# Block 0's attention computed transposed, and one written list of steps up to the 24th product

## The chip, the core and the metric

The kernel runs on one core of one Trainium2 chip. The metric is the device time of one execution in microseconds (us), the median of several runs. Inputs and outputs lie in the chip's main memory; the kernel moves them with DMAs into the on-chip memory, where five engines work side by side: TensorE (PE; its weight loads are PEld), VectorE (DVE), ScalarE (ACT), GpSimd (POOL) and SyncE (SP), which here issues nearly all DMAs. Each engine executes its own queue strictly in the order in which it was written, and waits on semaphores for the others.

## The reference

Three steps in a row over 8 batches x 576 rows = 4608 tokens of 512 numbers (8 heads of 64):

```
kv  = einsum('bhsd,bhse->bhde', k, v)        # 64 x 64 per batch and head
o   = einsum('bhsd,bhde->bhse', q, kv)
x   = o / sqrt(mean(o*o over 64) + 1e-6) * g_norm        # per token and head
xn  = x / sqrt(mean(x*x over 512) + 1e-6) * rms_g        # per token
y   = (silu(xn @ w_gate) * (xn @ w_val)) @ w_out         # 512 -> 1536 -> 512
out = relu(y @ w_in)**2 @ w_out2                         # 512 -> 2048 -> 512
```

All of it is float32. The two norms of one token need, per head, the sum of o*o and the sum of o*o*g_norm*g_norm; both factors are then one number per token and head.

## The kernel before, in words

**Tiles and stages.** The 4608 tokens are nine blocks of 512 (`NB`, `T`). Blocks are worked on in stages: blocks 0 and 1 first, then 2, then pairs; first all stages of the gated layer, then those of the second layer. In a stage a *product* is six matmuls of 128x128 weights with 512 tokens into one PSUM bank (`product`): every operand is split into a high and a low part, and three of the four combinations for two slices of the contraction are summed. After each product the kernel calls `tick()`, a counter in the program text by which all other work is placed between the products: `at(t, fn)` and `after(n, fn)` put a step at a tick, and `prep_q` holds the steps that prepare weights, taken one per tick or slower (`pace["prep"]`). The engines see only the order that results.

**The first stage** has no prepared weights yet. For each unit of 256 columns of the gate matrix (`g`) and of the value matrix (`v`) the steps of `prep_unit` load 1 MB of raw 64-bit words (`load`), turn them into float32 with two ScalarE instructions (`bits_1`, `bits_2`) and two VectorE instructions (`bits_3`, `bits_4`), split them (`hi` on ScalarE, `lo` on VectorE), and store the words and the split form for later (`words_out`, `put`). Units 0 to 5 are used straight from where they are made: four products to a unit. Products 1 to 24 are block 0 with units 0 to 5, products 25 to 48 block 1 with the same units.

**Block 0's attention** stands ahead of the first product. `kv_whole` sums k-v products of five row chunks in PSUM, `kv_out` copies them to `kvb`, `o_mm2` multiplies two q tiles of 128 tokens each by it (tokens on the partitions), ScalarE squares the result out of PSUM, GpSimd multiplies the squares by g_norm squared (`att_sg`), VectorE sums both over 64 columns (`att_sum`, eight instructions), forms the factors with some twenty small instructions (`att_m`, `att_r`) and multiplies (`att_y2`). `x1_T` turns each 128x128 piece with TensorE so that features lie on the partitions, `x_hi` and `x_lo` split it into the operand of the products. `keep(n)` issues n matmuls of the identity into an unused bank. Block 1's attention (`o_events(1, 1, 3, 22, True)`) is spread over ticks 1 to 24; its pieces are turned at ticks 22 and 23.

**The order around the change** in the old text: a few `prep_step()` calls (each is one time step of the list that `prep_first` makes of all units), the loads, and the calls above, one under the other at the end of `attn_moe_moe`; then the ticks. VectorE and ScalarE take what comes in that order; SP issues at most eight DMAs ahead, since each of its eight semaphores must have come back before it is used again.

## Time and profile before

| what | us |
|---|---|
| median of 3 runs | 1572.36 (1570.51 to 1572.75) |
| the profiled execution, its own time | 1572.19 |
| its span, first to last instruction | 1570.4 |
| TensorE busy in the span | 1560.2 (99%) |
| VectorE / ScalarE / GpSimd busy | 1182.2 / 727.3 / 62.9 |
| bytes moved by DMA | 463.99 MB, mean 295 GB/s |

The span starts with the first instruction; times "at 30.95" are us from there. A row of the timeline gives the start, the length, the engine, the line, the operation, what it writes and reads, and how many instructions are merged; in brackets stands how long the engine had nothing to do ahead of it and what ended that. A float32 matmul is two records in the trace, a product's matmul one, so one q tile pair of `o_mm2` (64 matmuls in the program's count, 32 of them to a tile) and one filler of `keep` show different counts in the two views. The granted clock is given as a share of 2.4 GHz: 0.50 is 1.2 GHz.

### The profile page before, as it was taken

The numbers are of one execution on the slowest core, as the hardware profiler recorded it, in microseconds if no ns is written. First come the engines' busy times: TensorE is split into PE (matmuls) and PEld (weight loads), VectorE is DVE, ScalarE is ACT, GpSimd is POOL, SyncE is SP. The second block draws the span as 40 slices with busy tenths as digits, with TensorE's granted clock in tenths as the row PEclk, the third lists the DMA queues.
The fourth block names the chain that finished last, engine by engine and source line by source line (L and its number), as shares of the span: only waits on it lengthen the run. The fifth ranks groups of instructions, "written<-read, shape, count | busy, mean of one in ns | idle before, by whom it ended". The sixth has DMA issues, their size and how long they took to land.

```text
span 1570.4 us, 23134 instructions
## 1 busy us (share of the span) xinstructions
PE 1560.2 (99%) x8800; PEld 1301.6 (83%) x8800; DVE 1182.2 (75%) x1594; ACT 727.3 (46%) x983; POOL 62.9 (4%) x50
## 2 busy tenths in 40 slices
...
GB/s 373 327 394 412 345 293 337 394 315 358 397 261 259 295 336 353 219 353 347 394 318 265 390 338 219 246 249 191 196 247 244 194 198 253 236 195 205 230 409 235
DMA packets 174926, 463.99 MB, mean 295 GB/s; under 512 B 14048, under 2 KB 47840, under 8 KB 170464
## 3 DMA queue, kind: packets, MB, share of 16 engines
...
q8 instruction: 70, 1.15, 0.3%
...
## 4 chain that ended last, share of the span: by engine, by line
PE 97%; DVE 1%; DMA 1%; ACT 0%; SPq 0%; issue 0%
PE c L807 55%; PE a L1070 21%; PE e L1070 10%; PE d L1070 5%; PE acc L1037 2%; PE ops L519 1%; PE kvps L457 1%; PE idle L1227 1%; DMA kvraw<-in_kv_dram 1%; DVE ws L231 0%; DVE wpw L176 0%; DVE wpw L170 0%; PE xps L628 0%; DVE ss L568 0%; DVE hr L883 0%; PE kvps L481 0%
## 5 line engine op out<-in xcount | busy, mean ns | idle before, releaser
L807 PE MATMUL c<-xo,wt 128*128 128x512 f32 (+1 forms) x3480 | 759.2, 379 | 0.0
L807 PEld LDWEIGHTS c<-xo,wt 128*128 128x128 f32 x3480 | 629.4, 188 | 122.9
L1070 PE MATMUL a<-ho,wt 128*128 128x512 f32 (+1 forms) x1536 | 334.1, 376 | 0.0
L715 ACT ACTIVATE ho<-hr 128x1024 fp32r<-128x1024 f32 (+1 forms) x230 | 230.8, 1006 | 204.1 <-PE a L1070 97.4
L716 DVE TENSOR_TENSOR ho<-hr,ho 128x1024 fp32r<-128x1024 f32 (+1 forms) x230 | 266.2, 1159 | 73.5 <-ACT ho L715 72.8
L1070 PEld LDWEIGHTS a<-ho,wt 128*128 128x128 f32 x1536 | 275.5, 188 | 52.8 <-DVE ho L716 0.4
L818 ACT ACTIVATE s<-c 128x512 f32<-128x512 f32 (+1 forms) x228 | 129.7, 573 | 183.7 <-PE c L807 183.3
L822 DVE TENSOR_TENSOR c<-c,s 128x512 f32<-128x512 f32 (+1 forms) x174 | 113.1, 650 | 81.0 <-PE c L807 75.7
L1070 PE MATMUL e<-ho,wt 128*128 128x512 f32 (+1 forms) x768 | 167.5, 376 | 0.0
L1070 PEld LDWEIGHTS e<-ho,wt 128*128 128x128 f32 x768 | 137.6, 188 | 26.4 <-DVE ho L716 0.3
L719 DVE TENSOR_TENSOR hr<-hr 128x1024 f32<-128x1024 f32 (+1 forms) x128 | 147.8, 1155 | 2.2
L807 PE MATMUL c<-xo,ws 128*128 128x512 f32 x576 | 135.1, 393 | 1.3 <-DVE ws L231 1.2
L807 PEld LDWEIGHTS c<-xo,ws 128*128 128x128 f32 x576 | 106.9, 188 | 25.1 <-DVE ws L231 2.0
L716 DVE TENSOR_TENSOR xo<-xr,xo 128x1024 fp32r<-128x1024 f32 (+1 forms) x58 | 67.0, 1158 | 39.5 <-ACT xo L715 39.3
L883 DVE TENSOR_TENSOR hr<-c,hr 128x512 f32<-128x512 f32 x108 | 74.7, 693 | 17.9 <-PE c L807 16.2
L1070 PE MATMUL d<-ho,wt 128*128 128x512 f32 (+1 forms) x384 | 85.0, 376 | 0.0
L1070 PEld LDWEIGHTS d<-ho,wt 128*128 128x128 f32 x384 | 68.9, 188 | 13.1
L829 DVE SCALAR_TENSOR_TENSOR hr<-c 128x512 f32<-128x512 f32 (+1 forms) x120 | 76.7, 639 | 4.0
L826 ACT ACTIVATE hr<-hr 128x512 f32<-128x512 f32 x54 | 34.2, 633 | 89.0 <-DVE hr L822 88.8
L878 ACT ACTIVATE r<-c 128x512 f32<-128x512 f32 (+1 forms) x40 | 22.1, 554 | 113.6 <-PE c L807 103.9
L231 DVE TENSOR_TENSOR ws<-wpl,ws 128x1024 fp32r<-128x1024 f32 (+1 forms) x44 | 49.6, 1128 | 31.3 <-ACT ws L224 31.0
L554 POOL TENSOR_TENSOR sq<-sq,gg_sb 128x512 f32<-128x512 f32 x32 | 49.6, 1549 | 553.7 <-ACT sq L540 538.3
...
## 6 DMA issues: line engine op xcount, KB each, us to landing
wt<-wd_g SPq DMA_DIRECT2D x150, 512.0 KB, 7.1
wt<-wd_i SPq DMA_DIRECT2D x140, 512.0 KB, 5.0
wt<-wd_p SPq DMA_DIRECT2D x140, 512.0 KB, 4.7
wt<-wd_o SPq DMA_DIRECT2D x96, 512.0 KB, 5.6
...
kvraw<-in_kv_dram SPq DMA_DIRECT2D x35, 512.0 KB, 7.4
...
```

What stands on the lines that cost most here:

```text
L231: nc.vector.tensor_tensor(out=t[:, :, 1, :], in0=quarters(st["sw"[1 - h]])[:, q], in1=t[:, :, 0, :].bitcast(F32), op=ALU.subtract)
L554: nc.gpsimd.tensor_tensor(out=heads(sg), in0=heads(sq), in1=gg_sb.rearrange("p (o d) -> p o d", o=1).to_broadcast([128, H, D]), op=ALU.mult)
L715: nc.scalar.activation(out=dst[:, 0], in_=src, func=AF.Copy)
L716: eng.tensor_tensor(out=dst[:, 1], in0=src, in1=dst[:, 0].bitcast(F32), op=ALU.subtract)
L719: eng.tensor_tensor(out=o, in0=x, in1=y, op=ALU.subtract)
L807: nc.tensor.matmul(ps, lhsT=w[:, a, kc * 128:(kc + 1) * 128], rhs=x[:, b, kc, :], start=(start and n == 0 and kc == 0), stop=(n == 2 and k ...
L818: nc.scalar.activation(out=t, in_=ps, func=AF.Copy)
L822: nc.vector.tensor_tensor(out=o, in0=ps, in1=t, op=ALU.add)
L826: nc.scalar.activation(out=hr, in_=c, func=AF.Silu)
L829: nc.vector.scalar_tensor_tensor(out=hr, in0=c, scalar=0.0, in1=c, op0=ALU.max, op1=ALU.mult)
L883: after(2, lambda: nc.vector.tensor_tensor(out=hr, in0=c, in1=hr, op=ALU.mult))
L1070: nc.tensor.matmul(ps, lhsT=w[e][:, a, d * 128:(d + 1) * 128], rhs=x[:, b, e, :], start=(i in (1, 2, 5) and q == 0 and e == 0 and a + b == 0),
```

## The change

**Transposed attention for block 0.** `ot` multiplies with kv as the stationary operand and q as the moving one, so that the result has features on the partitions and 128 tokens in the columns; no `x1_T` follows. ScalarE squares it (`sq`), VectorE copies it out of PSUM (`cp`). The new constant `w4` (128x4: a column of ones for either head, and g_norm squared for either head) is multiplied with the squares by TensorE (`s`), which gives both sums per token and head in one PSUM tile; GpSimd's four multiplications and VectorE's eight sums of block 0 are gone. The factors come out with tokens on the partitions, so ScalarE spreads them over 64 columns (`rb`, four instructions), TensorE turns them (`t`, 16 transposes), and VectorE multiplies (`x`). `x_hi` and `x_lo` then read the result from on-chip memory.

**One list.** `FIRST` names every step up to the 24th product, by engine queue order: the first string runs ahead of product 1, string k after product k. `first_op` carries a name out; `prep_first` no longer emits units 0 to 5, nor the first three steps of unit 6, and the other preparations start at tick 21 (`BEGIN_PREP`). The silu and multiply of products 1 to 24 (`s0.0`, `h0.0`, ...) are in the list as well. The fillers fall from 44 to 13. Block 1 keeps its form; its steps have other places, and its 16 transposes now stand together after product 23.

The core of the diff:

```
+BEGIN_PREP = 21
+EARLY = 6
+FIRST = (
+    "kv.0 kv.1 keep.5 km0.0 kv.2 keep.1 km0.1 kv.3 keep.1 km0.2 kv.4 q.0 keep.1 km0.3 q.1 km0.4 load.0 kvb.0 "
+    "keep.1 ot.0 ot.1 q.2 sq.0 q.3 cp.0 b1.0 gr keep.1 ot.2 kv.5 b2.0 ot.3 load.1 sq.2 b3.0 sq.1 s.2 sq.3 cp.2 "
+    "s.1 b4.0 s.3 kv.6 s.0 cp.3 hi.0 km1.0 kv.7 m.0 b1.1 keep.1 km1.1 kv.8 r0.0 b2.1 keep.1 km1.2 kv.9 r1.0 q.4 "
+    "keep.1 km1.3 cp.1 q.5 rb.0 km1.4 rb.3 lo.0 load.2 t.0 rb.1 t.3 kvb.1 x.0 t.1 rb.2 o1.0 x.3 xh0.0 x.1 q.6 "
+    "xh0.3 t.2 xl0.0 xh0.1 q.7 yc1.0 x.2 load.3 yc0.0 xl0.1",
+    "xh0.2 xl0.3 sqb.0 xl0.2",
+    "b1.2 out.0 b3.1",
+    "b2.2 b4.1",
+    "sqb.1 load.4 b3.2 hi.1 sg.1 o1.2 b1.3 lo.1 hf.1",
...
+    "h1.0 yb.1",
+    "yb.3 yb.0 put.5",
+    "yb.2 h1.1 tb.0 h2.0 tb.1 xh1.0 tb.2 xl1.0 tb.3 xh1.2",
+    "xh1.1 xl1.2 xh1.3 xl1.1 s2.1 xl1.3 h2.1 b1.6 b2.6",
+)
...
+            if n <= EARLY:
+                units.append({fn.__name__: fn for _, fn in steps})
+                steps = [x for x in steps if n == EARLY and x[1].__name__ not in ("load", "bits_1", "bits_2")]
...
+        elif what == "ot":
+            t, t_0["o", n] = q_t.pop(n), psum.tile([128, NP, 128], F32, tag=f"b{n}", name="oT")
+            for p in range(NP):
+                for r in HALF:
+                    nc.tensor.matmul(t_0["o", n][r, p, :], lhsT=kvb[0][r, p, :], rhs=t[r, p, :], start=True, stop=True)
...
+            for p in range(NP):
+                nc.tensor.matmul(t_0["s"][:, n, p, :], lhsT=t_0["sq"][:, n, p, :], rhs=w4, start=True, stop=True)
...
+            nc.scalar.activation(out=t_0["rb"][:, n], in_=rr.to_broadcast([128, NQ, 2, D]), func=AF.Copy)
...
+                nc.tensor.transpose(out=ps[:, c, :], in_=t_0["rb"][:, n, c].rearrange("t h d -> t (h d)"), identity=ident)
...
+            nc.vector.tensor_tensor(out=x, in0=t_0["t", n], in1=x, op=ALU.mult)
...
-        keep(14)
-        kv_new(0, psum, "b4")
-        for c in range(len(SC)):
-            kv_whole(0, c)
-            keep(1 if c < 4 else 0)
-        kv_out(0)
-        for i in (0, 2):
-            o_mm2(i, ((psum, f"b{i}"), (psum, f"b{i + 1}")))
...
-        keep(16)
...
-        o_events(1, 1, 3, 22, True)
+        for k, names in enumerate(FIRST):
...
+        at(BEGIN_PREP, lambda: pace.update(prep=1.0))
```

What it does to three queues. First SP, from its first DMA on (`kvraw`: k and v rows, 0.5 MB each, the fifth 0.25 MB; `qt`: a q tile, 0.25 MB; `wraw`: a raw weight unit, 1 MB). Before:

```order
L152 DMA wraw<-in_wg_dram 128x2048
L450 DMA kvraw<-in_kv_dram 128x1024 x4
L450 DMA kvraw<-in_kv_dram 64x1024
L1210 DMA gr_sb<-in_gr_dram 128x69
L508 DMA qt<-in_qt_dram 128x512 x4
L152 DMA wraw<-in_wv_dram 128x2048
L450 DMA kvraw<-in_kv_dram 128x1024 x4
L450 DMA kvraw<-in_kv_dram 64x1024
L508 DMA qt<-in_qt_dram 128x512 x4
L152 DMA wraw<-in_wg_dram 128x2048
```

Now:

```order
L492 DMA kvraw<-in_kv_dram 128x1024 x4
L492 DMA kvraw<-in_kv_dram 64x1024
L550 DMA qt<-in_qt_dram 128x512 x2
L186 DMA wraw<-in_wg_dram 128x2048
L550 DMA qt<-in_qt_dram 128x512 x2
L759 DMA gr_sb<-in_gr_dram 128x69
L492 DMA kvraw<-in_kv_dram 128x1024
L186 DMA wraw<-in_wv_dram 128x2048
L492 DMA kvraw<-in_kv_dram 128x1024 x3
L492 DMA kvraw<-in_kv_dram 64x1024
L550 DMA qt<-in_qt_dram 128x512 x2
L186 DMA wraw<-in_wg_dram 128x2048
```

The first weight unit moved from ahead of the first k and v rows to behind them and two q tiles; batch 1's rows and the next units moved forward.

Second TensorE, from its start to its first product (`idle`: the fillers; `kvps`: sums of k and v; `ops`: `o_mm2`; `xps`: `x1_T`; `c`: products). Before:

```order
L457 MATMUL kvps<-kvraw 64x64 x8
L519 MATMUL ops<-kvb_101,qt 64x64 x64
L1227 MATMUL idle<-ident 128x128 x16
L457 MATMUL kvps<-kvraw 64x64 x8
L1227 MATMUL idle<-ident 128x128 x2
L457 MATMUL kvps<-kvraw 64x64 x8
```

Now, the whole stretch from the last chunk of batch 0 on:

```order
L499 MATMUL kvps<-kvraw 64x64 x16
L762 MATMUL idle<-ident 128x128
L774 MATMUL oT<-qt,kvb_101 64x128 x16
L762 MATMUL idle<-ident 128x128
L774 MATMUL oT<-qt,kvb_101 64x128 x16
L787 MATMUL sums<-w_124,sq 128x4 x16
L499 MATMUL kvps<-kvraw 64x64 x8
L762 MATMUL idle<-ident 128x128
```

The row of 16 fillers between the batches is gone; the sums stand there, and one filler instead of two follows each chunk of batch 1.

Third VectorE, the same stretch (`ss`: sums of squares; `m`, `r`, `a`: the factors; `wpw`, `ws`: weight words and split weights). Before:

```order
L170 SCALAR_TENSOR_TENSOR wpw<-wps,wpw 128x1024
L176 SCALAR_TENSOR_TENSOR wpw<-wps,wpw 128x1024
L231 TENSOR_TENSOR ws<-wpw,ws 128x4x256
L568 TENSOR_REDUCE ss_416<-sq 128x8 x2
L568 TENSOR_REDUCE ss_417<-y 128x8
L568 TENSOR_REDUCE ss_416<-sq 128x8
```

Now:

```order
L782 COPY xt<-oT 128x4x128
L204 SCALAR_TENSOR_TENSOR wpw<-wps,wpw 128x1024
L782 COPY xt<-oT 128x4x128
L210 SCALAR_TENSOR_TENSOR wpw<-wps,wpw 128x1024
L782 COPY xt<-oT 128x4x128
L622 TENSOR_SCALAR m<-sums 128x32
L623 RECIPROCAL ss_337<-m 128x32
```

Ahead of the factors VectorE has three copies and two instructions for the first weights, where it had three for the weights and eight sums.

## Rows read from the trace of the kernel before

**Rows 1.** The page: busy time of each engine, share of the span, instructions.

```profile
PE 1560.2 (99%) x8800; PEld 1301.6 (83%) x8800; DVE 1182.2 (75%) x1594; ACT 727.3 (46%) x983; POOL 62.9 (4%) x50
```

**Rows 2.** Who waited for whom, TensorE, whole span: us in total, times, longest.

```profile
PE c L807 <- DVE ws L231: 1.2, 2, 0.9
```

**Rows 3.** Timeline of TensorE, 0 to 73: start, length, what, count [idle before].

```profile
1.36 6.06 PE L1227 MATMUL idle<-ident 128*128 128x128 f32 x28 [1.36 <-POOL ident masks.py:199]
...
13.44 2.96 PE L519 MATMUL ops<-kvb,qt 64*64 64x64 f32 x107 [0.48 <-ACT kvb L499]
...
30.95 1.72 PE L807 MATMUL c<-xo,ws 128*128 128x512 f32 x6
32.60 1.16 PE L519 MATMUL ops<-kvb,qt 64*64 64x64 f32 x64
...
65.94 1.23 PE L628 MATMUL xps<-ident,y 128*128 128x128 f32 x8
...
72.13 1.15 PE L457 MATMUL kvps<-kvraw 128*64 128x64 f32 x32
73.21 13.89 PE L807 MATMUL c<-xo,ws 128*128 128x512 f32 x60
```

**Rows 4.** Windows: length, busy PE, PEld, DVE, ACT, POOL (counts), clock, DMA share, GB/s.

```profile
14.00:15.00 1.00, 1.00 (x48) 1.00 (x44) 0.00 (x0) 0.00 (x0) 0.00 (x0) 0.50 1.07 447
...
21.00:22.00 1.00, 1.00 (x12) 1.00 (x10) 0.87 (x3) 0.51 (x1) 0.93 (x1) 1.00 1.01 381
...
42.00:44.00 2.00, 2.00 (x69) 1.70 (x69) 2.00 (x2) 1.01 (x3) 1.96 (x2) 1.00 0.44 107
```

**Rows 5.** The chain that ended last, 0 to 75: start, length, what.

```profile
2.83 8.36 DMA kvraw<-in_kv_dram
```

**Rows 6.** Timeline of ScalarE, the front.

```profile
5.64 1.13 ACT L160 ACTIVATE wps<-wraw 128x1024 f32<-128x1024 f32 x1 [3.41 <-DMA wraw<-in_wg_dram]
6.67 1.23 ACT L164 ACTIVATE wpw<-wraw,floor 128x1024 int32<-128x1024 uint8 x1
...
15.18 1.09 ACT L1247 ACTIVATE sq<-ops 128x512 f32<-128x512 f32 x2 [1.80 <-PE ops L519]
...
29.92 2.43 ACT L650 ACTIVATE xo<-xps,gg_rg 128x512 fp32r<-128x512 f32 x4 [0.68 <-PE xps L628]
```

**Rows 7.** Timeline of VectorE, the front.

```profile
22.57 0.17 DVE L574 TENSOR_SCALAR m<-ss 128x32 f32<-128x32 f32 x1
...
25.94 2.48 DVE L621 TENSOR_TENSOR y<-ops,r 128x512 f32<-128x512 f32 x4
...
30.64 2.73 DVE L654 SCALAR_TENSOR_TENSOR xo<-xps,gg_rg,xo 128x512 fp32r<-128x512 f32 x4 [1.08 <-ACT xo L650]
```

**Rows 8.** Groups of VectorE's instructions, 30.9 to 72.2: count, busy, mean ns, idle before.

```profile
L176 DVE SCALAR_TENSOR_TENSOR wpw<-wps,wpw 128x1024 int32<-128x1024 int32 x5 | 7.6, 1525 | 0.0
L231 DVE TENSOR_TENSOR ws<-wpw,ws 128x1024 fp32r<-128x1024 f32 x5 | 6.7, 1334 | 3.2 <-ACT ws L224 3.2
L170 DVE SCALAR_TENSOR_TENSOR wpw<-wps,wpw 128x1024 int32<-128x1024 int32 x5 | 6.6, 1325 | 0.0
...
L883 DVE TENSOR_TENSOR hr<-c,hr 128x512 f32<-128x512 f32 x5 | 3.4, 681 | 0.0
L568 DVE TENSOR_REDUCE ss<-sq 128x8 f32<-128x256 f32 (+1 forms) x8 | 3.4, 470 | 0.0
L616 DVE TENSOR_TENSOR y<-y,r 128x512 f32<-128x512 f32 x4 | 2.5, 684 | 0.0
```

**Rows 9.** DMAs issued 169 to 170: KB each, us from issue to landing.

```profile
wt<-wd_o SPq DMA_DIRECT2D x1, 512.0 KB, 6.2
```

**Rows 10.** Timelines 110 to 178: ScalarE, SP, then TensorE.

```profile
145.11 1.12 ACT L160 ACTIVATE wps<-wraw 128x1024 f32<-128x1024 f32 x1 [5.24 <-DMA wraw<-in_wo_dram]
...
169.39 3.49 SPq L418 DMA_DIRECT2D wt<-wd_o  x4
...
177.32 5.60 PE L1070 MATMUL a<-ho,wt 128*128 128x512 f32 x24
```

More of the change, by code (lines that the diff above doesn't have):

```diff
@@ L275, in prep_unit @@
         bits_3.landed = lambda: now[0] >= begin
-        bits_1.landed = lambda: kind == "words" or late(st["t"])
+        bits_1.landed = lambda: late(st["t"])
         if kind == "sums":
@@ L327, in prep_units, with prep_first @@
         )
-    def prep_first(units, raws):
+    units = []
+    def prep_first(plan, raws):
         raws, events = cycle(raws), []
-        outs = {(key, h): at for key, _, _, _, places in units for h, at in enumerate(places)}
-        for n, (key, kind, base, room, places) in enumerate(units):
+        outs = {(key, h): at for key, _, _, _, places in plan for h, at in enumerate(places)}
+        for n, (key, kind, base, room, places) in enumerate(plan):
             ahead = 7 if n == 0 else 10 if n == 1 else 5 if kind == "words" else base - FIRST_LOAD[key[1]]
@@ L545, in att_c2 @@
             att_new(j)
-        for h, ps in enumerate(o_ps.pop(i)):
-            nc.scalar.activation(out=two(y_t[j], c, h), in_=ps, func=AF.Copy)
+        for h in hs:
+            nc.scalar.activation(out=two(y_t[j], c, h), in_=o_ps[i][h], func=AF.Copy)
     def two(t, c, h):
@@ L694, in o_events @@
[L694 to L706 removed]
+            at(u + 1 + n, lambda n=n: att_r(j, n))
@@ L872, in done @@
                 hr = raw[q, b][:, g if e is None else e, :]
-                if layer == 2:
+                if first[0] and n < 3 and b[1] == "1":
+                    name = f"{'sh'[g]}{n}.{int(b[0]) - 1}"
+                    fn = (lambda: gate(hr, c)) if g == 0 else lambda: nc.vector.tensor_tensor(out=hr, in0=c, in1=hr, op=ALU.mult)
+                    jobs[name] = fn
+                    at(keys[name], lambda: first_op(name))
+                elif layer == 2:
                     if sbuf:
@@ L1187, in attn_moe_moe @@
         ]
-        preps = [prep_first(units, stgs), prep_units([(key, "sums") for key in gv[:6]], 5, hops, xts[:3], stgs + xts[:2:-1])]
+        preps = [prep_first(plan, stgs), prep_units([(key, "sums") for key in gv[:6]], 5, hops, xts[:3], stgs + xts[:2:-1])]
         h_preps = {}
```

224 lines of the change are left out of this document (125 added, 99 removed), and 16 rows, old and new, of the table FIRST.

## The prediction

> **What bounds the kernel now.** I read the page first. TensorE is busy in 99% of the span [rows 1], so only its idle time and work that need not be there can go. Next, who waited for whom on TensorE: the one wait in its products is 1.2 us, for a split weight [rows 2]; the same view restricted to what follows 72 us names no wait at all. The timeline of TensorE says where the rest is: fillers and attention up to 30.95, where block 0's first product starts, two thirds of block 1's attention behind it, and at 72.13, after the 25th product, the first work for block 2 [rows 3]. From there to the end, some 1500 us, it is one closed row of work that the change leaves as it is. So the sum has one term that counts: how much earlier than 72.13 the 25th product ends, and whether that lead is kept. It is made against the profiled execution's 1572.19; the median is 0.17 above it.
>
> **Part 1, data ahead of the first product.** DMAs land one after the other. The first raw unit of 1 MB was there at 5.64 [rows 6], the fourth k-v chunk at 2.83 + 8.36 = 11.19 [rows 5]: 1.4 us for a chunk of 0.5 MB, about 2.7 for 1 MB. The change puts that unit behind batch 0's chunks, so the fourth lands near 8.5, the short fifth near 9.2. Before, TensorE began with kv 13.44 - 11.19 = 2.2 us after the fourth chunk [rows 3, 5]; now near 10.7. Two q tiles land by 10.5, the unit at 13.1, the other two tiles at 14.4.
>
> **Part 2, the transposed attention.** No row shows the new matmul. For two tiles it has 16 matmuls of 128 columns where the old had 64 of 64 columns. From below it costs what the old form does, 1.16 for two tiles [rows 3], 0.6 each; from above eight fillers of the same 128 columns, two records each, 12 records to the us at full clock [rows 4]: 1.4. It uses half as many corners of the array at a time, so I take 0.9. The fourth tile is ready near 15.5. ScalarE converts the unit first, 1.13 + 1.23 from 13.1 [rows 6], then squares: three times 0.55 [rows 6], to 17.0. The new sums are 16 matmuls of four columns; at most a filler's 0.17 each, at least nothing beside their weights' loads; I take 0.1, and the last two groups end at 17.8. VectorE is later than that: two weight instructions (1.2 each, a little under the means of [rows 8]) and two copies at the price of an old PSUM read, 2.48 / 4 [rows 7], take it from 15.4 to 19.0. Then come the same factors as before, 25.94 - 22.57 = 3.4 [rows 7], to 22.4, where before they were ready at 25.94. The eight sums and GpSimd's four multiplications are no longer ahead of them.
>
> What is new behind them: ScalarE spreads the first quarter (0.6), TensorE turns it (four transposes, at most 0.6) once batch 1's last chunk is in; by Part 1's pace that lands at 23.0 and is summed by 23.7. So VectorE multiplies from 24.3, three times 0.65 to 26.3, and ScalarE's split of the second piece (2.43 / 4 [rows 6]) ends near 27.0. **The first product starts at 27.0** instead of 30.95, and the `ops` of 1.16 that stood behind it [rows 3] are ahead of it, beside VectorE's multiplications.
>
> **Part 3, 27.0 to the 25th product.** TensorE needs 23 products at 6 x 13.89 / 60 = 1.39 [rows 3] and one pair of `ops`, 33.0 us, until it wants block 1's transposes. VectorE stands at 27.0 + 2.5 when its split of block 0 (2.73 / 4 each [rows 7]) is done. From there to the last scaled row of block 1 it has five units' 15 weight instructions, 7.6 + 6.7 + 6.6 us with the delays that they showed beside GpSimd, the sums (3.4), factors (3.4), four multiplies (2.7) and scalings (2.5) [rows 7, 8]: 32.9, some 1.4 less since one instruction starts before the last has ended. That is 27.0 + 34.0, so TensorE waits about 1 us there: VectorE is what is late next. The old 3.2 us that VectorE waited for a split in this stretch [rows 8] have no place in the new order, since units 2 to 5 are loaded earlier. The 16 transposes (the half of them took 1.23 [rows 3], together I put 1.9) and two products (2.8) follow: 27.0 + 38.7 = 65.7. **At full clock the point comes 6.4 us earlier.** SP's new order costs nothing that I can find: the writes of the split weights move behind the loads, and the window 42 to 44, in which the DMAs were busy to 0.44 [rows 4], is room for them.
>
> **Part 4, the clock.** The records grant 0.50, that is 1.2 GHz, in 14 to 15, though TensorE was busy all of that slice [rows 4]; it had done small matmuls with pauses before. It was back at 1.00 by 21 [rows 4], after the row of fillers. The first 28 records took 6.06 us [rows 3], half the later pace, so the start ran slow too. Of 44 fillers 13 stay. At half clock the old `ops` took 2.96 / 107 us a record, at full clock 1.16 / 64 [rows 3]: half as long again. The cost is between 0 (nothing slow on the path) and about 8: four tiles at 1.75 push the sums to 20; five chunks with their fillers at 1.9 instead of 1.0 (as DMA brings them, 1.3) push the last chunk from 23.7 to 29.5; `ops` and transposes 0.6 more; then the first products lose half of what they do at half clock, of which I count 1.7. Nearest is the drop that the trace shows: one stretch, slow at 14 and over at 21, of which a part falls on waits for data. I take 2.4, a third of the way.
>
> The Trainium skill speaks against the change here: TensorE: Matmul & The Clock Gate, section "What's actually happening", says that the throttled state is the default and only activity releases it. By it the front would be slow throughout, and the sum would be the slow rival's below; the trace agrees in so far as the front's first fillers ran at half pace.
>
> **Sum:** 1572.19 - 6.4 + 2.4 = 1568.2, with the median's 0.17 **1568.3**.
>
> **Rivals.**
> *Slow front.* The clock stays at 1.2 GHz from the start into the first products: 6.4 - 8 = 1.6 us lost, **1573.8** and up. It decides once the last chunk of batch 1 is summed later than about 27. For it: the drop at 14 happened with more fillers than now. Against: the four q tiles follow each other without a pause when slow, and after such a row the clock came back. 13 in 100.
> *The lead is lost at the third matrix.* At 177.32 TensorE takes weights whose DMA was issued at 169.39 and landed 6.2 later [rows 9, 10]: 1.7 us of room. They can be read back only when SP has written the last unit, behind VectorE, and ScalarE waited 5.24 us for a raw unit that landed at 145.1 [rows 10]. If DMAs, not TensorE's pace, hold that chain, only 1.7 us stay: **1570.5**. Against it: SP's loads wait for TensorE in many places and move with it, and the DMAs had gaps before (42 to 44). 17 in 100.
> *Full clock.* The pauses are too short for a drop: 1572.36 - 6.4 = **1566.0**, between 1564.3 and 1566.8. 20 in 100.
> *My forecast*, one slow stretch, lead kept: 1566.8 to 1570.2, 45 in 100. What is left, 5 in 100, is some wait of the list that I have not seen.
>
> **How the numbers follow.** A measurement of this kernel can tell some 0.2% from no change, 3.1 us. Faster by more, below 1569.2: the full-clock case and about 38 of my 45, so 0.58. Slower by more, above 1575.5: half of the slow front and a part of the unseen, 0.07. Between: 0.35. The range 1564.3 to 1573.5 takes in the forecast, the full-clock case, the lost lead and the near part of the slow front; it leaves out about 12 in 100.
>
> **What would show it.** The factors' first instruction near 19 to 20, where it was 22.57; the first product between 27 and 30; no wait in products 1 to 23 over 0.5 us; a wait of about 1 us before the transposes, ended by VectorE; `kvps` of block 2 near 68 and then every later landmark earlier by the same amount, the third matrix included (173.3 for 177.32). A granted clock of 0.50 for about 7 us of the first 35. It is wrong if the first product comes after 31, if the landmark at 177.32 moves less than the one at 72.13, or if weights hold up the products.

## The result, and the profile after

| | before | after |
|---|---|---|
| median of the runs | 1572.18 us (4 runs, 1570.51 to 1572.75) | 1583.55 us (4 runs, 1579.27 to 1585.0) |
| profiled execution | 1572.19 | 1582.92 |
| its span | 1570.4 | 1580.4 |

The ratio is 1.007, with a 95% interval of 1.0048 to 1.0091: **0.7% slower, 11 us**. The forecast was 4 us faster, its range ended at 1573.5. Direction and range were both wrong.

The page's busy times of the changed kernel. TensorE has 94 instructions fewer than in [rows 1] and is busy 4.7 us longer in a span that is 10 us longer, so it now also waits more.

```profile
PE 1564.9 (99%) x8706; PEld 1303.4 (82%) x8706; DVE 1183.7 (75%) x1590; ACT 729.0 (46%) x987; POOL 63.1 (4%) x51
```

Who waited for whom, changed kernel, TensorE. In [rows 2] one line had 1.2; here the longest is 3.5, for weights that come back from DRAM by DMA.

```profile
PE a L1193 <- DMA wt<-wd_o: 3.5, 1, 3.5
PE c L927 <- DVE ws L265: 1.7, 2, 1.2
PE kvps L499 <- DMA kvraw<-in_kv_dram: 1.4, 3, 0.6
...
PE c L927 <- ACT hr L946: 0.8, 1, 0.8
```

The timeline of TensorE, changed kernel (start, length, what, count, [idle before]). Against [rows 3] and [rows 10]: the first product is at 33.37 (before 30.95), `kvps` of block 2 at 74.95 (72.13), the third matrix at 184.45 (177.32).

```profile
4.30 1.12 PE L499 MATMUL kvps<-kvraw 128*64 128x64 f32 x16 [0.43 <-DMA kvraw<-in_kv_dram]
...
13.23 3.68 PE L774 MATMUL oT<-qt,kvb 64*64 64x128 f32 x32
16.84 0.79 PE L762 MATMUL idle<-ident 128*128 128x128 f32 x2
17.57 1.97 PE L774 MATMUL oT<-qt,kvb 64*64 64x128 f32 x32
19.47 3.74 PE L787 MATMUL sums<-w,sq 128*128 128x4 f32 x32
23.13 0.69 PE L499 MATMUL kvps<-kvraw 128*64 128x64 f32 x16
...
27.52 2.17 PE L499 MATMUL kvps<-kvraw 128*64 128x64 f32 x32
29.63 2.31 PE L800 MATMUL rps<-ident,rb 128*128 128x128 f32 x12
...
33.37 1.47 PE L927 MATMUL c<-xo,ws 128*128 128x512 f32 x5
...
70.33 1.91 PE L676 MATMUL xps<-ident,y 128*128 128x128 f32 x16
...
74.95 1.15 PE L499 MATMUL kvps<-kvraw 128*64 128x64 f32 x32
...
184.45 7.33 PE L1193 MATMUL a<-ho,wt 128*128 128x512 f32 x24 [3.55 <-DMA wt<-wd_o]
```

Three things to see. The four tiles' `oT`: the first two take 3.68, the next two, the same work, 1.97, so the pace up to about 17.6 was half. The sums take 3.74 in one closed row. And the third matrix waits 3.55 and then takes 7.33 for 24 records that took 5.60 in [rows 10].

Windows of the changed kernel (columns as in rows 4; clock, DMA share and GB/s last): half clock in two stretches, the front's second one and the one behind the wait for weights. The slow pace up to 17.6 does not show in this column (see the last section).

```profile
24.00:31.00 7.00, 7.00 (x77) 5.96 (x77) 4.09 (x15) 2.96 (x6) 0.00 (x0) 0.53 1.03 385
...
184.90:188.20 3.30, 3.30 (x10) 2.53 (x9) 1.60 (x2) 0.00 (x0) 0.00 (x0) 0.50 0.98 359
```

Where the 10.7 us between the profiled executions lie: 2.8 up to `kvps` of block 2 (74.95 against 72.13); 4.3 more up to the third matrix (184.45 - 177.32 = 7.1), of which 3.55 is the wait for its weights; 1.7 in its first 24 records (7.33 - 5.60, half clock); 1.9 behind it and outside the span. So six of the eleven are lost 110 us after the end of the list that the change wrote.

The link between the two is SP's queue. First the timeline of SP in the changed kernel and one row of its ScalarE, then the window 31 to 55 of the kernel before and of the changed one.

```profile
25.72 0.33 SPq L221 DMA_DIRECT2D wf_g<-wpw  x1
38.12 0.33 SPq L186 DMA_DIRECT2D wraw<-in_wg_dram  x1
42.03 0.33 SPq L186 DMA_DIRECT2D wraw<-in_wv_dram  x1
...
60.44 6.65 SPq L273 DMA_DIRECT2D wd_g<-ws  x4
...
177.04 3.64 SPq L457 DMA_DIRECT2D wt<-wd_o  x4
```

```profile
36.85 1.25 ACT L198 ACTIVATE wpw<-wraw,floor 128x1024 int32<-128x1024 uint8 x1
```

Kernel before:

```profile
31.00:55.00 24.00, 24.00 (x224) 19.50 (x223) 20.73 (x24) 19.70 (x27) 12.29 (x10) 1.00 0.94 340
```

Changed kernel:

```profile
31.00:55.00 24.00, 22.42 (x217) 17.34 (x216) 23.10 (x23) 19.67 (x26) 14.52 (x8) 0.99 0.58 205
```

Between 25.72 and 38.12 SP issues nothing: the next entry, `load.4`, waits for a raw buffer, that is for `b2.2`, which ScalarE runs at 36.85 and ends at 38.10. The writes of split weights (`wd_g<-ws`), ready from 28 on, stand far behind it in the list and go out in a heap from 56 to 72. The DMAs were busy to 0.58 instead of 0.94: (0.94 - 0.58) x 24 = 8.6 us of DMA time that did not move anything. The third matrix's first weight tile landed at 177.04 + 7.3 = 184.3, before at 169.39 + 6.2 = 175.6 [rows 9, 10]: 8.7 us later. That the two numbers are nearly equal does not make one the whole cause of the other: e1 below gives most of the 8.6 back and moves the third matrix by 3.3. DMAs of the changed kernel issued 177.0 to 177.3 (KB each, us to landing):

```profile
wt<-wd_o SPq DMA_DIRECT2D x1, 512.0 KB, 7.3
```

### The profile page after: what moved, and what is told of

It is laid out like the page before. It is cut to its first block, busy times and chain, and to the rows that moved or that the text cites. A ratio compares the mean times of both kernels' runs of the same rounds, so it can differ in the third digit from the quotient of the medians.

```text
span 1580.4 us, 22942 instructions
## 1 busy us (share of the span) xinstructions
PE 1564.9 (99%) x8706; PEld 1303.4 (82%) x8706; DVE 1183.7 (75%) x1590; ACT 729.0 (46%) x987; POOL 63.1 (4%) x51
## 4 chain that ended last, share of the span: by engine, by line
PE 88%; DMA 4%; DVE 3%; issue 2%; POOL 1%; ACT 1%; SPq 0%; POOLq 0%; DVEq 0%; ACTq 0%
PE c L927 50%; PE a L1193 20%; PE e L1193 10%; PE d L1193 5%; PE acc L1160 2%; DMA kvraw<-in_kv_dram 1%; DMA wd_g<-ws 1%; PE ops L561 1%; PE kvps L499 1%; DVE ws L265 1%; DMA wf_v<-wpw 1%; DMA wraw<-in_wo_dram 1%; POOL sq L604 1%; DMA wt<-wd_o 0%; DVE ho L836 0%
## 5 line engine op out<-in xcount | busy, mean ns | idle before, releaser
L1193 PEld LDWEIGHTS d<-ho,wt 128*128 128x128 f32 x384 | 68.9, 188 | 13.1
L265 DVE TENSOR_TENSOR ws<-wpl,ws 128x1024 fp32r<-128x1024 f32 (+1 forms) x44 | 49.6, 1128 | 30.3 <-ACT ws L258 30.1
```

The source lines that it names most:

```text
L265: nc.vector.tensor_tensor(out=t[:, :, 1, :], in0=quarters(st["sw"[1 - h]])[:, q], in1=t[:, :, 0, :].bitcast(F32), op=ALU.subtract)
L1193: nc.tensor.matmul(ps, lhsT=w[e][:, a, d * 128:(d + 1) * 128], rhs=x[:, b, e, :], start=(i in (1, 2, 5) and q == 0 and e == 0 and a + b == 0),
```

## The experiments

Theory A: the list's order on SP leaves the DMAs idle, they never catch up, and the third matrix pays. Theory B: the late front is the loss, and the rest follows from it. Landmarks of the profiled executions and medians of all runs (the kernel before, run beside them, had medians from 1571.5 to 1572.3):

| kernel | first product | `kvps` block 2 | third matrix [wait] | median, us | ratio to before (95%) |
|---|---|---|---|---|---|
| before | 30.95 | 72.13 | 177.32 [-] | 1572.2 | |
| change | 33.37 | 74.95 | 184.45 [3.55] | 1583.55 | 1.0070 (1.0048 to 1.0091) |
| e1 writes early | 33.40 | 75.00 | 181.14 [0.78] | 1577.28 | 1.0033 (1.0021 to 1.0044) |
| e2 46 fillers | 35.31 | 76.89 | 186.02 [3.79] | 1582.70 | 1.0073 (1.0060 to 1.0087) |
| e3 no halving | 36.16 | 76.07 | 186.68 [4.15] | 1580.69 | 1.0046 (1.0032 to 1.0060) |
| e4 all three | 35.34 | 75.29 | 181.31 [0.67] | 1577.56 | 1.0034 (1.0022 to 1.0047) |
| e5 e1, reordered | 33.79 | 73.64 | 179.88 [0.89] | 1576.35 | 1.0030 (1.0018 to 1.0042) |
| e6 e5, no halving, no fillers between batch 1's chunks | 32.53 | 73.34 | 179.38 [0.69] | 1575.23 | 1.0019 (1.0010 to 1.0029) |
| e7 e6, fillers at the start | 35.04 | 73.18 | 178.98 [0.45] | 1574.65 | 1.0016 (1.0006 to 1.0025) |
| e8 sums twice | 40.58 | 82.19 | 192.11 [4.57] | 1588.76 | 1.0108 (1.0087 to 1.0128) |
| e9 e6, reordered further | 31.82 | 70.81 | 176.79 [0.63] | 1573.20 | 1.0009 (1.0001 to 1.0018) |
| e12 e9, next steps earlier | 33.36 | 72.11 | 179.04 [1.58] | 1574.74 | 1.0018 (1.0008 to 1.0027) |

### e1: the writes of split weights earlier on SP

```diff
-    "b1.2 out.0 b3.1",
+    "b1.2 out.0 put.0 b3.1",
...
-    "sqb.1 load.4 b3.2 hi.1 sg.1 o1.2 b1.3 lo.1 hf.1",
+    "sqb.1 out.1 load.4 b3.2 hi.1 sg.1 o1.2 b1.3 lo.1 hf.1",
...
-    "load.5 b3.3 hi.2 b1.4 hf.0",
+    "load.5 put.1 b3.3 hi.2 b1.4 hf.0",
...
-    "yc0.2 sv.0 out.3 hi.3 b3.4 q.8 q.9",
+    "yc0.2 sv.0 put.2 out.3 hi.3 b3.4 q.8 q.9",
...
-    "h0.0 out.4 sg.3 b2.5 su.3",
+    "h0.0 out.4 put.3 sg.3 b2.5 su.3",
```

> The changed kernel with put.0 to put.3 and out.1 moved to an earlier place in the list (SP's queue): the writes of split weights go out when the weights are ready, ahead of loads that have to wait. Theory A (SP's order leaves the DMAs idle between 31 and 50, the backlog then makes the third matrix's weights late): DMA share of 35 to 50 rises from a mean of 0.49 to over 0.7, the first wt DMA of the third matrix is issued some 4 us before 177.04, TensorE's wait of 3.55 at 184.45 falls below 1, the granted clock stays at 1.00 behind it (1.73 back), first product unchanged at 33.4: 1577 to 1579, from 1583.6. Theory B (the late front alone is the loss, 2.8 at 74.95, and the rest is its consequence): the wait at 184.45 stays above 3 and the time within 1.5 us of 1583.6.

Five DMAs changed their place in one queue, and 6.3 us came back between the medians (4.8 between the two profiled spans). Window of this run, then SP's first weight DMAs of the third matrix and that matrix on TensorE:

```profile
31.00:55.00 24.00, 22.38 (x216) 17.34 (x215) 23.03 (x23) 19.77 (x26) 14.50 (x8) 0.99 0.88 329
```

```profile
174.29 3.84 SPq L457 DMA_DIRECT2D wt<-wd_o  x4
```

```profile
181.14 5.70 PE L1193 MATMUL a<-ho,wt 128*128 128x512 f32 x24 [0.78 <-DMA wt<-wd_o]
```

The DMA share of 31 to 55 is 0.88 (0.58 in the change). First product and `kvps` did not move (33.40, 75.00), which is what tells A from B: the wait went from 3.55 to 0.78, and the 24 records behind it are back at 5.70, so the half clock there was a consequence of the wait. The first weight DMA was issued at 174.29 instead of 177.04, 2.75 earlier and not the 4 expected. The DMAs make up a part of what they lose: ScalarE could start on that matrix's first raw unit 7.0 earlier than in the change (81.32 for 88.35), TensorE on the matrix only 3.3 earlier (181.14 for 184.45). The other 5 us over the kernel before are not SP's five writes.

### e2: more fillers in the changed kernel

```diff
-    "kv.0 kv.1 keep.5 km0.0 kv.2 keep.1 km0.1 kv.3 keep.1 km0.2 kv.4 q.0 keep.1 km0.3 q.1 km0.4 load.0 kvb.0 "
+    "kv.0 kv.1 keep.14 km0.0 kv.2 keep.2 km0.1 kv.3 keep.2 km0.2 kv.4 q.0 keep.2 km0.3 q.1 keep.1 km0.4 load.0 kvb.0 "
...
-    "keep.1 km1.3 cp.1 q.5 rb.0 km1.4 rb.3 lo.0 load.2 t.0 rb.1 t.3 kvb.1 x.0 t.1 rb.2 o1.0 x.3 xh0.0 x.1 q.6 "
+    "keep.4 km1.3 cp.1 q.5 rb.0 keep.2 km1.4 rb.3 lo.0 load.2 t.0 rb.1 t.3 kvb.1 x.0 t.1 rb.2 o1.0 x.3 xh0.0 x.1 q.6 "
```

Likewise 3, 3 and 6 fillers around the four tiles and 3 and 4 ahead of `km1.1` and `km1.2`: 46 in all, for 13. The expectation counts them as 39, by mistake.

> The changed kernel with 39 fillers ahead of the first product instead of 13 (14 at the start, the rest in the pauses): no other step is moved. Theory A: the granted clock is 1.00 from about 7 on with at most one short drop, the first product comes at 29.5 to 31 instead of 33.37 and kvps of block 2 at 71 to 72.5 instead of 74.95, but the third matrix's weights still land near 184, so that its wait grows from 3.55 to some 6 and the time stays between 1581 and 1584. Theory B: all of the 2.5 to 4 us come back at the end too: 1579 to 1581. Rival: the pauses are for data and squares, not for the clock, and the first product comes later than 32 whatever the clock.

The rival's number came (later than 32), but its "whatever the clock" was not tested. TensorE ran at full pace from 6.2 on, yet the clock fell again in the sums, and the fillers of batch 1, now at half pace, pushed the last chunk and the first product back by 2. The time is the change's within its interval. Timeline of TensorE, then the window:

```profile
18.99 4.37 PE L787 MATMUL sums<-w,sq 128*128 128x4 f32 x32
23.29 1.12 PE L499 MATMUL kvps<-kvraw 128*64 128x64 f32 x16
...
35.31 1.71 PE L927 MATMUL c<-xo,ws 128*128 128x512 f32 x5
```

```profile
20.00:24.00 4.00, 4.00 (x38) 3.98 (x39) 1.37 (x4) 3.17 (x3) 0.00 (x0) 0.71 1.03 334
```

### e3: no adding of halves on GpSimd

```diff
-    "sqb.1 load.4 b3.2 hi.1 sg.1 o1.2 b1.3 lo.1 hf.1",
+    "sqb.1 load.4 b3.2 hi.1 sg.1 o1.2 b1.3 lo.1",
...
-    "load.5 b3.3 hi.2 b1.4 hf.0",
+    "load.5 b3.3 hi.2 b1.4",
...
-    "su.0 out.1 s1.1 b3.5 hf.2 hi.4 load.6",
+    "su.0 out.1 s1.1 b3.5 hi.4 load.6",
```

> The changed kernel without GpSimd's hf.0 to hf.2 (the adding of halves of block 1's squares): VectorE sums full 64 columns for three more tiles, the result is the same up to rounding. If GpSimd beside it is what slows VectorE's weight instructions (2.23, 1.75, 1.75, 2.00 in 40 to 48 instead of 1.2 to 1.5) then those beside the removed work return to 1.2 to 1.5, GpSimd is done near 50 instead of 58.5, the waits of TensorE before products (0.53, 0.85, 1.22) fall by half in sum and kvps of block 2 comes 1 to 2 us before 74.95. If not, VectorE has 1 us more of sums and kvps comes 0 to 1 later. The time, by theory A, moves by under 1 us either way, since DMAs set the third matrix.

Groups of VectorE's instructions, 38 to 60, in the changed kernel, then in this one:

```profile
L210 DVE SCALAR_TENSOR_TENSOR wpw<-wps,wpw 128x1024 int32<-128x1024 int32 x5 | 7.9, 1588 | 0.0
L265 DVE TENSOR_TENSOR ws<-wpw,ws 128x1024 fp32r<-128x1024 f32 x3 | 5.4, 1814 | 0.0
L610 DVE TENSOR_REDUCE ss<-sq 128x8 f32<-128x256 f32 x6 | 2.5, 411 | 1.3 <-POOL sq L604 1.3
```

```profile
L210 DVE SCALAR_TENSOR_TENSOR wpw<-wps,wpw 128x1024 int32<-128x1024 int32 x5 | 7.2, 1431 | 0.0
L265 DVE TENSOR_TENSOR ws<-wpw,ws 128x1024 fp32r<-128x1024 f32 x3 | 4.7, 1552 | 0.0
L610 DVE TENSOR_REDUCE ss<-sq 128x8 f32<-128x512 f32 x6 | 3.9, 670 | 0.0
```

VectorE's weight instructions are shorter, its sums longer by 0.26 each, and its wait for GpSimd is gone. GpSimd itself ended at 58.1 and not near 50, as its last multiplications came later. From the first product to `kvps` of block 2 it is 76.07 - 36.16 = 39.9, against 74.95 - 33.37 = 41.6: 1.7 less, in the range expected. The total cannot show it: in the profiled execution the front's data came later (TensorE waited 3.9 for k-v chunks, 1.4 in the change), and the five runs spread from 1577.1 to 1586.4.

### e4: the three together

The edits of e1, e2 and e3; where two meet in one line:

```diff
-    "load.5 b3.3 hi.2 b1.4 hf.0",
+    "load.5 put.1 b3.3 hi.2 b1.4",
...
```

> The three edits together (writes early, 39 fillers, no halving). By theory A they add up, since the front's gain is no longer taken by the weights: first product 29.5 to 31, kvps of block 2 at 69 to 72, third matrix at 175 to 178 with a wait under 1: 1568 to 1573. By theory B 1577 to 1579, since the writes give nothing. Rival: VectorE is late behind TensorE's earlier products and the waits for split weights grow by what the front gives: 1574 to 1577.

1577.56 with the edits of e1 to e3, the same as e1 alone. The wait for weights is 0.67. The fillers cost the front what the missing halving gave behind it (`kvps` 75.29 for 75.00). The expectation of 1568 to 1573 was wrong, as the fillers did not help.

### e5: VectorE's pause, ScalarE's order, later loads earlier

```diff
-    "keep.1 km1.3 cp.1 q.5 rb.0 km1.4 rb.3 lo.0 load.2 t.0 rb.1 t.3 kvb.1 x.0 t.1 rb.2 o1.0 x.3 xh0.0 x.1 q.6 "
-    "xh0.3 t.2 xl0.0 xh0.1 q.7 yc1.0 x.2 load.3 yc0.0 xl0.1",
-    "xh0.2 xl0.3 sqb.0 xl0.2",
-    "b1.2 out.0 b3.1",
-    "b2.2 b4.1",
-    "sqb.1 load.4 b3.2 hi.1 sg.1 o1.2 b1.3 lo.1 hf.1",
+    "keep.1 km1.3 cp.1 q.5 rb.0 km1.4 rb.3 lo.0 b3.1 b4.1 load.2 t.0 rb.1 t.3 kvb.1 x.0 t.1 rb.2 o1.0 x.3 xh0.0 x.1 q.6 "
+    "xh0.3 t.2 xl0.0 xh0.1 q.7 b1.2 x.2 load.3 xl0.1",
+    "xh0.2 xl0.3 xl0.2 b2.2 hi.1",
+    "out.0 put.0 out.1 yc1.0",
+    "yc0.0 sqb.0",
+    "sqb.1 load.4 b3.2 sg.1 o1.2 b1.3 lo.1 hf.1",
...
-    "yc0.2 sv.0 out.3 hi.3 b3.4 q.8 q.9",
+    "yc0.2 sv.0 put.2 load.6 out.3 hi.3 b3.4 q.8 q.9",
...
-    "lo.4 sv.3 put.2",
+    "lo.4 sv.3 b1.6 b2.6",
...
-    "xh1.1 xl1.2 xh1.3 xl1.1 s2.1 xl1.3 h2.1 b1.6 b2.6",
+    "xh1.1 xl1.2 xh1.3 xl1.1 s2.1 xl1.3 h2.1",
```

`put.1` and `put.3` stand as in e1, and `out.1` leaves its old place.

> Beyond the early writes: b3.1 and b4.1 go into VectorE's pause behind lo.0 (2.45 us before the first multiplication), so out.1 can leave at 31; b1.2, b2.2 and hi.1 stand ahead of the copies of the second pair of block 1's tiles on ScalarE; load.6 goes ahead of the q and k-v loads of product 9, and b1.6, b2.6 from the end of the list to product 18, where ScalarE idles (61 to 71), so that the third matrix's raw units follow earlier. Theory A (the backlog of DMAs sets the third matrix): DMA share of 35 to 40 from 0.40 to over 0.8, load of wo's first unit issued near 66 to 70 instead of 76.4, and the third matrix no longer waits for weights (0.78 in the run with early writes, 3.55 in the change); the waits in the products (0.5, 0.9, 1.2) shrink to under 1 in sum, so that kvps of block 2 comes 1.5 to 2.5 before 75.0. Time 1573.5 to 1576, from 1577.3. If the DMAs were no longer the bound behind the early writes: only the gain in the products, and the third matrix waits no more than before. If it stays at 1577, the third matrix is held by something later than 100 us.

`kvps` came 1.36 earlier than in e1 and the waits in the products went from 2.6 to 1.0, a little less than expected; the wait for weights stayed (0.89), where none was expected: the third matrix moved with its weights, by 1.26, and the median by 0.9. That fits theory A's bound at a smaller size.

### e6: no halving, no fillers in batch 1

```diff
-    "s.1 b4.0 s.3 kv.6 s.0 cp.3 hi.0 km1.0 kv.7 m.0 b1.1 keep.1 km1.1 kv.8 r0.0 b2.1 keep.1 km1.2 kv.9 r1.0 q.4 "
-    "keep.1 km1.3 cp.1 q.5 rb.0 km1.4 rb.3 lo.0 b3.1 b4.1 load.2 t.0 rb.1 t.3 kvb.1 x.0 t.1 rb.2 o1.0 x.3 xh0.0 x.1 q.6 "
+    "s.1 b4.0 s.3 kv.6 s.0 cp.3 hi.0 km1.0 kv.7 m.0 b1.1 km1.1 kv.8 r0.0 b2.1 km1.2 kv.9 r1.0 q.4 "
+    "km1.3 cp.1 q.5 rb.0 km1.4 rb.3 lo.0 b3.1 b4.1 load.2 t.0 rb.1 t.3 kvb.1 x.0 t.1 rb.2 o1.0 x.3 xh0.0 x.1 q.6 "
```

This against e5, with e3's edit as well.

> The last kernel, without halving, and without the three fillers between the chunks of batch 1 (0.8 us each at half clock in 25 to 29.6). If the pace of TensorE at half clock sets the front there, the last chunk is summed near 28 instead of 29.6 and the first product comes at 31.5 to 32.5 instead of 33.4; if the data set it (last chunk landed at 26.85) it is the same. kvps of block 2 at 70.5 to 72.5, time 1571 to 1574, about that of the kernel before.

In this profile the clock stayed up, and the chunks were as fast as their data. Timeline of TensorE, then the window:

```profile
25.45 0.69 PE L499 MATMUL kvps<-kvraw 128*64 128x64 f32 x16 [0.29 <-DMA kvraw<-in_kv_dram]
26.59 0.68 PE L499 MATMUL kvps<-kvraw 64*64 64x64 f32 x16 [0.45 <-DMA kvraw<-in_kv_dram]
...
32.53 0.50 PE L927 MATMUL c<-xo,ws 128*128 128x512 f32 x1 [1.15 <-ACT xo L698]
```

```profile
24.00:31.00 7.00, 5.80 (x150) 4.84 (x147) 6.55 (x18) 3.30 (x6) 0.00 (x0) 1.00 1.04 367
```

The last chunk was summed at 27.3 instead of 30.1 in e5, but the first product came only 1.3 earlier than in e5, since ScalarE's `b1.2` now stood ahead of a split that TensorE needed (1.15). `kvps` of block 2 (73.34) and the median (1575.23) missed the expected ranges, although the clock stayed up in the run profiled: the half clock alone is not what is left. Ten runs spread from 1572.28 to 1577.82, against 1570.64 to 1573.39 in 21 runs of the kernel before.

### e7: fillers at the start only

```diff
-    "kv.0 kv.1 keep.5 km0.0 kv.2 keep.1 km0.1 kv.3 keep.1 km0.2 kv.4 q.0 keep.1 km0.3 q.1 km0.4 load.0 kvb.0 "
-    "keep.1 ot.0 ot.1 q.2 sq.0 q.3 cp.0 b1.0 gr keep.1 ot.2 kv.5 b2.0 ot.3 load.1 sq.2 b3.0 sq.1 s.2 sq.3 cp.2 "
+    "kv.0 kv.1 keep.14 km0.0 kv.2 keep.2 km0.1 kv.3 keep.2 km0.2 kv.4 q.0 keep.2 km0.3 q.1 keep.1 km0.4 load.0 kvb.0 "
+    "keep.3 ot.0 ot.1 q.2 sq.0 q.3 cp.0 b1.0 gr keep.3 ot.2 kv.5 b2.0 ot.3 load.1 sq.2 b3.0 sq.1 s.2 sq.3 cp.2 "
```

This against e6.

> The last kernel with the many fillers at the start and up to the fourth tile (as in the run with 39), none in batch 1. If the many small matmuls of the sums (4 columns each) take the clock down by themselves, the records show half clock from about 20 to 27 even behind a stretch at full clock, and the first product comes within 1 us of the last kernel's. If pauses took it down, it stays at 1.00 and the first product comes at 30 to 31.

The clock fell behind the sums all the same, in spite of a full pace from 6 to 23, with one longer wait (1.36 for a q tile, up to 17.36). The first product (35.04) was 2.5 later than in e6, whose clock had stayed up. Window of this run:

```profile
24.00:31.00 7.00, 4.92 (x66) 4.29 (x63) 6.42 (x17) 3.71 (x7) 0.00 (x0) 0.55 1.04 336
```

Median and spread (1571.41 to 1578.69) are e6's. So what decides whether the front's second stretch is slow was not found by placing fillers: e6, with ten of them, kept its clock in the one execution that was profiled.

### e8: the sums twice

```diff
-            for p in range(NP):
+            for p in [*range(NP)] * 2:
```

> The changed kernel with each of the 16 sums matmuls issued twice (same result). If their 0.23 us each lie on the path, as the profile shows them in one closed row of 3.74, VectorE's first factor instruction comes 2.5 to 3.7 later than 23.24 and the first product 1.5 to 3.7 later than 33.37. By the prediction's 0.1 each it would be 1.6 later at most; if squares or copies set the factors, nothing moves.

Timeline of TensorE, then of VectorE:

```profile
18.44 10.08 PE L787 MATMUL sums<-w,sq 128*128 128x4 f32 x64 [0.22 <-POOL w L1341]
```

```profile
28.56 0.19 DVE L622 TENSOR_SCALAR m<-sums 128x32 f32<-128x32 f32 x1 [8.27 <-PE sums L787]
```

16 more matmuls of four columns cost 10.08 - 3.74 = 6.3. The row began 1.0 earlier (18.44 for 19.47), so the factors started 5.3 later (28.56 for 23.24) and the first product 7.2 later, both more than I had bounded. The factors begin where the sums end: the sums are on the path with their whole length. The extra ones cost 0.39 each and not 0.23: the window 22 to 24 of this run has a granted clock of 0.64, the next two 0.50, so the second half ran slow, and the front stayed slow behind it. In all 5.2 us between the medians, of two runs here.

### e9: four more moves

```diff
-    "s.1 b4.0 s.3 kv.6 s.0 cp.3 hi.0 km1.0 kv.7 m.0 b1.1 km1.1 kv.8 r0.0 b2.1 km1.2 kv.9 r1.0 q.4 "
+    "s.1 b4.0 s.3 kv.6 s.0 cp.3 hi.0 lo.0 km1.0 kv.7 m.0 b1.1 km1.1 kv.8 r0.0 b2.1 km1.2 kv.9 r1.0 q.4 "
...
-    "xh0.3 t.2 xl0.0 xh0.1 q.7 b1.2 x.2 load.3 xl0.1",
-    "xh0.2 xl0.3 xl0.2 b2.2 hi.1",
+    "xh0.3 t.2 xl0.0 xh0.1 q.7 x.2 load.3 xl0.1",
+    "xh0.2 b1.2 xl0.3 xl0.2 b2.2 hi.1",
...
-    "sqb.1 load.4 b3.2 sg.1 o1.2 b1.3 lo.1",
-    "b2.3 b4.2 sg.0",
-    "load.5 put.1 b3.3 hi.2 b1.4",
+    "sqb.1 load.4 b3.2 sg.1 o1.2 b1.3 lo.1 put.1",
+    "b2.3 b4.2 out.2 sg.0",
+    "load.5 b3.3 hi.2 b1.4",
```

This against e6.

> The kernel without fillers in batch 1 (e6), with four more moves: lo.0 into VectorE's pause ahead of the factors, b1.2 behind xh0.2 on ScalarE (it made TensorE wait 1.15 + 0.72), put.1 and out.2 ahead of load.5 on SP. Theory A (the list's order on SP, ScalarE and VectorE holds what is left): first product 1 to 2 earlier than 32.53 where the clock stays up, the wait of 1.62 for a split weight falls under 0.8, kvps of block 2 at 71 to 72.5, third matrix at 177.5 to 179: 1571 to 1574. If what is left is the front's clock alone, the median stays at 1574 to 1576 and the runs spread over 5 as in e6. Better than the kernel before by over 0.2% it can hardly be, since its third matrix still comes no earlier than 177.3.

1573.20, inside the expected range, 0.1% above the kernel before. Timeline of TensorE, then the window:

```profile
31.82 1.44 PE L927 MATMUL c<-xo,ws 128*128 128x512 f32 x5
...
70.81 1.15 PE L499 MATMUL kvps<-kvraw 128*64 128x64 f32 x32
...
176.79 5.69 PE L1193 MATMUL a<-ho,wt 128*128 128x512 f32 x24 [0.63 <-DMA wt<-wd_o]
```

```profile
31.00:55.00 24.00, 23.73 (x195) 18.64 (x184) 20.28 (x24) 20.36 (x27) 6.95 (x4) 1.00 1.01 374
```

With the DMAs busy to 1.01 and the split weights in time, `kvps` of block 2 is 1.3 *earlier* than in the kernel before, although the half clock was there (0.52 in 24 to 31). Of that lead the third matrix keeps 0.5, since its weights land at 176.7, later than before (175.6). Here DMA time in 31 to 55 is no longer what holds those weights; what does was not found (e12). The attention in transposed form is not what costs 11 us: with it, and by order, fillers and halving alone, 11.4 over the kernel before become 1.7, each median against the runs beside it.

### e10: more DMA in the kernel before

```diff
+            if key == ("v", 2) and kind == "words":
+                for extra in idle_dma:
+                    nc.sync.dma_start(out=extra, in_=src[f].rearrange("p u n -> p (u n)").bitcast(I32))
```

> The kernel before with three more DMAs of 1 MB each behind the load issued at 42.34 (DRAM to DRAM, into scratch that nobody reads; result unchanged). They stand for a stretch in which the queue moves nothing that is needed. At the price of a 1 MB load, 2.7 each, 8 us of DMA time. Theory A: before 177 the DMAs are what is short (busy to 0.95 and more from 50 on), so the third matrix's weights land some 6 to 8 later than 175.6, TensorE's lead of 1.7 is used up and it waits 4 to 7 at 177.32; the front and kvps of block 2 at 72.13 move by under 1.5: 1576 to 1580. Theory B (TensorE and VectorE set that stage, DMAs have room): the third matrix moves by under 1.5 and the time stays under 1574.

The time came as theory A had it (1578.18, ratio 1.0039, 1.0023 to 1.0054), the place did not. Timeline of TensorE, then a row of ScalarE:

```profile
67.36 5.49 PE L811 MATMUL c<-xo,ws 128*128 128x512 f32 x12 [4.89 <-ACT ws L228]
...
184.07 5.60 PE L1074 MATMUL a<-ho,wt 128*128 128x512 f32 x24
```

```profile
61.01 1.21 ACT L168 ACTIVATE wpw<-wraw,floor 128x1024 int32<-128x1024 uint8 x1 [6.42 <-DMA wf_g<-wpw]
```

In the old order the three DMAs held up a write that ScalarE waits for (6.42 us until 61.01), and through it a split weight of the products: 4.89 on TensorE, and half clock behind it (12 records in 5.49, 2.8 at the pace of [rows 3]). The third matrix then had no wait, as TensorE itself came 6.75 later. So DMA time that is missing between 42 and 60 can cost TensorE, but which consumer pays, and how much the clock adds, depends on the order. The link from the change's idle DMAs to the third matrix rests on e1, not on this run.

### e11: 13 fillers in the kernel before

```diff
-        keep(14)
+        keep(5)
...
-        keep(16)
+        keep(1)
...
-            keep(2 if c < 4 else 0)
+            keep(1 if c < 3 else 0)
...
-        keep(2)
```

> The kernel before with 13 fillers instead of 44 (5 at the start, one after each of the first four chunks, one ahead of batch 1's chunks, three between them), nothing else moved: the price of the fillers in the old form. If the fillers held the clock up, TensorE works at half pace for 7 to 14 us more of the first 35, the last chunk of batch 1 is summed later than 28.8 or the row of ops takes longer, and the first product comes 1 to 4 later than 30.95: 1573.5 to 1576. If VectorE (factors ready at 25.94, four scalings to 28.4) and the data set the front there, the first product stays within 0.5 of 30.95 or comes up to 1 earlier, and the time within 1.5 of the kernel before's.

Timeline of TensorE:

```profile
6.97 1.12 PE L457 MATMUL kvps<-kvraw 128*64 128x64 f32 x16 [3.11 <-DMA kvraw<-in_kv_dram]
...
29.46 0.55 PE L628 MATMUL xps<-ident,y 128*128 128x128 f32 x2 [3.54 <-DVE y L621]
...
33.52 2.91 PE L807 MATMUL c<-xo,ws 128*128 128x512 f32 x6
```

The fillers had a price in the old form: 1575.18, ratio 1.0018 (1.0009 to 1.0027), 3.5 us between the medians and 2.8 by the ratio. Batch 0's chunks ran at 1.12 instead of 0.69; the last chunk of batch 1 was summed earlier than before, at 25.9, but then TensorE waited 3.54 for VectorE and the first products ran at half pace (2.91 for six records, 1.72 in rows 3).

### e12: what follows the list two products earlier

```diff
-BEGIN_PREP = 21
+BEGIN_PREP = 19
```

> The reordered kernel (e9) with the steps that follow the list begun two products earlier (19 instead of 21), so that the raw unit 7 is converted some 2.8 earlier on ScalarE and the load of wo's second unit leaves some 2 to 3 before 76.32. Theory A: the share of the DMAs in 75 to 100 rises from 0.88 to over 0.92, the third matrix's weights land 0.6 or more before 176.66, its wait of 0.63 goes and the whole is 0.5 to 1.5 faster than e9's 1573.2: 1571.7 to 1572.7, the same as the kernel before. If DMAs between 100 and 175, where they are busy to 0.99 and more, are all that counts, no change against e9.

A miss. The share of the DMAs in 75 to 100 is 0.90 (0.88 in e9), the wait for weights 1.58 (0.63), the median 1574.74 with runs from 1572.0 to 1576.7. In its profile the front was 1.5 slower than in e9's. No version that I ran beats the kernel before.

## Why the prediction was wrong

It was wrong in three steps, and the one that an experiment isolates best was one sentence.

**"SP's new order costs nothing that I can find"** (Part 3). It cost 6.3 us between the medians, shown by e1, which moves five DMAs in SP's queue and nothing else. I had seen that the writes of split weights move behind the loads, and covered them with room in the window 42 to 44 [rows 4]. I knew that SP issues in order, but did not follow its new list: an entry that waits stops all that stand behind it. `load.4` waits for ScalarE's `b2.2`, which the list puts behind block 0's splits and block 1's copies, at 36.85. So the raw unit 4 was loaded at 38.12, later than before (34.54), where Part 3 had counted on earlier loads. The cover I named was idle time of the DMAs in the old order; in the new one DMAs stood idle because the queue did. The rival "the lead is lost at the third matrix" named the place, but priced it as a lead that shrinks to 1.7 us. It assumed that the DMAs' own pace would stay; the weights landed 8.7 us later, and TensorE waited 3.55 there and lost 1.73 more to the clock behind the wait. e1 gave 2.77 of the wait and 1.63 of the clock's part back.

**The sums at 0.1 each** (Part 2). Their 16 matmuls took 3.74, 0.23 each, above the 0.17 that I gave as the upper end; e8 shows that the length is on the path. The upper end was misread: the 12 records that [rows 4] counts in 21 to 22 include some that began before it. In the trace the fillers' records start 0.11 apart there, so a filler of two records is 0.22, and the records of the sums start 0.11 apart as well: they cost what a filler costs. The factors began at 23.24 and not at 19.0. Of these 4.2, 2.1 are the size of the sums (3.74 for 1.6); the rest stood ahead of them, as the fourth tile was ready at 19.5 and not at 15.5. `oT` at full pace was near its size, 1.97 for two tiles against 1.8.

**The clock at 2.4** (Part 4) and the data that went with it. The start ran at half pace up to 17.6, not to some 7, and a second slow stretch followed from about 24.4 to 31.3. The chunk at 4.30 took 1.12, the one at 23.13 took 0.69. The Trainium skill (TensorE: Matmul & The Clock Gate, "What's actually happening") says that the throttled state is the default and that activity releases it, which I had read as a front slow throughout; the trace agrees up to 17.6 and not from there to 24.4. Going from 44 fillers to 13 alone cost some 3 in the old form (e11); putting them back into the changed kernel gave nothing (e2). The last chunk of batch 1 landed later than Part 1 had it, at 15.7 + 11.1 = 26.8 instead of 23.0 (DMAs issued 11 to 18, KB each, us to landing):

```profile
kvraw<-in_kv_dram SPq DMA_DIRECT2D x1, 256.0 KB, 11.1
```

The pace of 1.4 per chunk did not hold: already the fourth chunk was there at 10.3 and not at 8.5, and the first raw unit at 15.0 and not at 13.1. At half pace TensorE reached that last chunk only after it had landed (its row at 27.52 has no wait), so the clock, more than the data, set when it was summed. The first product came at 33.37: 6.4 later than the 27.0 of the sum, of which the clock's 2.4 had allowed for a part. "It is wrong if the first product comes after 31" was met, and so was "if weights hold up the products" (1.7 in two waits).

**Part 3's length** was nearer. From the first product to `kvps` it took 41.6 where I had 38.7. 1.8 of the difference are waits: 0.21, 0.53, 0.85 and 1.22 for VectorE and ScalarE, where I expected one of 1 before the transposes. Beside GpSimd's halving the splits (L265) took 1.81 each, not the 1.33 of [rows 8]; e3 gives 1.7 of the 2.9 back.

Against the sum: forecast -4.0, profiled execution +10.7, so 14.7 were missed. 6.8 lie ahead of `kvps` (68.1 forecast with the clock, 74.95), which is the sums, the clock, the data and the waits of Part 3 together; 4.3 between there and the third matrix and 1.7 in its half clock, which is mostly SP's order; 1.9 behind it and outside the span.

Open: why the clock fell behind the sums or in them, between 21.7 and 25.2, in every profiled execution of the new form but e6's. The sums are the work just ahead of it, and TensorE was busy in all of 20 to 24 (4.00 us) in the changed kernel, but no run was made with the sums taken out, and the old form, which has none, shows a drop too (0.50 at 14 in [rows 4], 29.6 in e11). Open as well: what holds the third matrix's weights in e9, where they still land 1.1 later than in the kernel before.
